# The head of a delta-rule and GELU kernel: a root on ScalarE, first squares on VectorE, unread products ahead of K, Q one tile ahead, loads in another order

## The chip, the core and the metric

The kernel runs on one core of a Trainium2 chip. The metric is the time of one execution on the device in microseconds (us); lower is better. The core has a matrix engine (TensorE, PE in the profile), a vector engine (VectorE, DVE), an engine for functions of one operand (ScalarE, ACT), a general one (GpSimd, POOL), and a queue that starts most transfers (SyncE, SP). Each engine takes its instructions in program order; semaphores order them between engines. Transfers run on 16 DMA engines.

## What is computed

```python
def _attn_ref(q, k, v, beta):                 # 4 x 8 heads, 768 tokens, 48 wide
    k_n = k / (np.linalg.norm(k, axis=-1, keepdims=True) + 1e-06)
    state = 0; y = 0
    for t in range(S):
        kt, vt, bt = (k_n[:, :, t], v[:, :, t], beta[:, :, t, None])
        y[:, :, t] = np.einsum('bhd,bhde->bhe', q[:, :, t], state)
        v_old = np.einsum('bhde,bhd->bhe', state, kt)
        state = state + bt[:, :, :, None] * np.einsum('bhd,bhe->bhde', kt, vt - v_old)
    return y

def _moe_ref(x, w_in, w_out):                 # x: 3072 tokens of 384; hidden 2048
    h = x @ w_in
    g = 0.5 * h * (1.0 + erf(h / sqrt(2)))
    return g @ w_out
```

q, k, v and beta are single precision. The two weight matrices come in double precision and are turned to single precision on the chip. The attention's output, with its heads joined, is the x of the second part.

## The kernel before

**Tiles.** The 768 tokens are cut into 12 chunks of 64 (`NC`, `C`). A unit (`tiles[c, a]`) holds chunk c of two batches, one in each half of the 128 partitions, all 8 heads side by side; a is 0 or 1, so there are two units a chunk. Two chunks form a group g, which is worked on as a whole where a small triangular system has to be inverted: the 64 x 64 block of a head is cut into 32 x 32 blocks, and the diagonal blocks are inverted by an elimination over 31 rows (`eliminate_steps`, L494).

**The head.** The first four units (`first`, chunks 0 and 1) are the first group. The order of their work is written out by hand on all five engines (L1189 to L1284); behind it a plan of due times (L1301 to L1425) orders VectorE and GpSimd. What happens, step by step:

- Loads: K of the four units, half of each on SP's queue and half on ScalarE's (L170, L171), then beta, then Q (L176), V of chunk 0 (`load_v(0)`, L1193), weight parts 0 and 1 (`fetch`, L1195), K of chunk 2 (`load_k`, L1196), and later Q of chunk 2, K of chunk 3, weight parts 2 and 3, the first three parts of the second matrix (L1232, into the `w_raw` slots) and V of chunk 1 (L1234).
- Norms: `squares` (L333) squares K and sums over 48 elements, on VectorE for three units and on GpSimd for one. `root` (L388) takes the square root of the 128 x 32 sums on VectorE: a start value out of the bits of the number and three Newton steps of three instructions. `factors` (L325) turns the root and beta into the factor `gm` of each token and head.
- K transposed (`transposed(u, (0,))`, L408): four TensorE transposes into PSUM and one ScalarE copy, L423. `diagonals` (L479) multiplies the transposed K with itself for the 32 x 32 diagonal blocks and copies them out on ScalarE (L492). `signs` (L1180) does the same for beta.
- `scales` (L498) transposes `gm` on VectorE (`gt`, L501) and spreads it on GpSimd into XM (L504). `flip` (L509) transposes the diagonal blocks of all four units into Nu (L511), and Nu is multiplied by XM (L516). The elimination, 58 small instructions on VectorE and some at its ends, works on Nu. Two transposes (`back`, L542 and L545) put the result into XM and Zf.
- While VectorE eliminates, TensorE and ScalarE do early work: `grams` (L448) of the four units, beta of the later chunks, Q transposed and `queries` (L466) for one unit after the other, then K transposed, grams and Q transposed for chunk 2 (`third`), and K and grams of chunk 3 (`fourth`). ScalarE also sums the squares of chunk 2 by head (`sum_of_squares`, L351: 16 instructions).
- After the elimination: `join` (L565) in two levels, `solve` (L776, products psU), `use` (L804, psY), `read`, `turn`, then the first products of the second part (`fc1`, L898, psH).

**Weights.** Sixteen parts are turned to single precision, each by `begin`, `exponents`, `mantissas` and `signed`. The exponent takes one of two forms (`two_kinks`, L240): one with two ScalarE passes and no sign step on VectorE, or one with a single ScalarE pass and one VectorE instruction more (L284). `signed` starts the transfer of the part that takes the freed place. There are four places for the parts of the first matrix (`NS`), and three for those of the second.

**Buffers.** PSUM tiles are "sq" (transposes, two buffers), "dn" (two of two banks each) and "mlp" (two).

Of the kernel before, what the change touches and what calls it, by code (L numbers as in the profile page):

```python
# [19 lines left out]
def kernel(  # L20
# [65 lines left out]
    lim = cpool.tile([128, 4], F32)  # L86
    for i, x in enumerate((-896.0 * 2 ** 23, 0.0, -896.0 - 1792.0 / 4095.0, 128.0 * 1792.0 / 4095.0)):
        nc.vector.memset(lim[:, i:i + 1], x)
# [69 lines left out]
    def load_v(c):  # L158
        if c >= NC:
            return  # L160
        for a in range(NA):
            u = tiles[c, a]
            u.V = io.tile([128, H, D], F32, tag="V", name="V", bufs=4)
            fetch_in(u.V, v, u)
# [17 lines left out]
    for i in range(NKS):  # L182
        nc.gpsimd.memset(Kp[i][:, :, D:], 0.0)
    mask = cpool.tile([128, C], F32)
    Gp = [cpool.tile([128, NA, NF, 128], F32, name=f"G{i}") for i in range(2)]
    G = Gp[0]
# [4 lines left out]
    nc.gpsimd.memset(mask, 1.0)  # L191
    nc.gpsimd.memset(low, 1.0)
    nc.gpsimd.affine_select(out=low, in_=low, compare_op=ALU.is_ge, fill=0.0, base=-1,
                            pattern=[[1, HB], [-1, HB]], channel_multiplier=0)
    for p in range(2):
        nc.gpsimd.affine_select(out=mask[HALF[p]], in_=mask[HALF[p]], compare_op=ALU.is_ge,
                                fill=0.0, base=-1, pattern=[[1, C]], channel_multiplier=-1)
    half = cpool.tile([128, NA * H], F32)
    nc.gpsimd.memset(half, 0.5)
    mask_h = mask.unsqueeze(1).to_broadcast([128, H, C])  # L200
    Zf = [cpool.tile([128, NU, C], F32, name="Zf")] * 2
    for p in range(2):
        nc.vector.memset(Zf[0][p * C + HB:(p + 1) * C, :, 0:HB], 0.0)
# [3 lines left out]
    nc.scalar.activation(lim[:, 1:2], lim[:, 0:1], ACT.Gelu)  # L207
# [32 lines left out]
    def two_kinks(n):  # L240

        return 0 < n < n_in or n_in + 3 < n < n_in + 7
# [79 lines left out]
    def new_group(g):  # L322
        gms[g] = wk.tile([128, 2 * NA, H], F32, tag="gm", name="gm")
# [9 lines left out]
    def squares(u, n, engine=None):  # L333
        kd = u.Kn[:, :, 0:D]
        if engine is nc.gpsimd:
            ksq = su.tile([128, H, D], F32, tag="w_e", name="ksq")
        elif engine is None:
            if u.c < 8:
                u.ksq = early_pair[u.a]
            else:  # L340
                if u.a == 0:
                    ns["ksq"] = more[0].tile([128, NA, H, D], F32, tag="TX", name="ksq")
                u.ksq = ns["ksq"][:, u.a]
            keep(nc.scalar.activation, u.ksq, kd, ACT.Square)
            return
        else:
            ksq = early_sq
        engine.tensor_tensor(ksq, kd, kd, op=ALU.mult)
        nc.vector.tensor_reduce(n, ksq, axis=AX.X, op=ALU.add)
# [12 lines left out]
    def norms(c):  # L362
        us = [tiles[c, a] for a in range(NA)]
        g = c // 2
        if c % 2 == 0:
            new_group(g)
        if c > 3 and c % 2 == 0:
            n = ns["pair"] = wk.tile([128, 2 * NA, H], F32, tag="n", name="n")
            ns[c], ns[c + 1] = n[:, 0:NA], n[:, NA:]
        for u in us:  # L370
            if c > 3:
                squares(u, None)
# [15 lines left out]
    def root(x):  # L388

        shape = list(x.shape)  # L390
        s = wk.tile(shape, F32, tag="root", name="root", bufs=1)
        r = wk.tile(shape, F32, tag="root_r", name="root_r", bufs=1)
        nc.vector.tensor_scalar(s.bitcast(U32), x.bitcast(U32), 0.5, 532487669.0,
                                op0=ALU.mult, op1=ALU.add)
        nc.vector.tensor_scalar_mul(x, x, 0.5)
        for i in range(3):
            nc.vector.reciprocal(r, s)
            nc.vector.tensor_tensor(r, r, x, op=ALU.mult)
            nc.vector.scalar_tensor_tensor(x if i == 2 else s, s, 0.5, r, ALU.mult, ALU.add)
# [603 lines left out]
    def keep(fn, *args, **kw):  # L1003
        i = fn(*args, **kw)  # L1004
        if free:
            tc.keep_in_program_order(i)
# [173 lines left out]
    def signs(c0, c1):  # L1180
# [11 lines left out]
        mybir.EngineType.PE, mybir.EngineType.SP}))  # L1192
    load_v(0)  # L1193
    for n in range(2):
        fetch(n)  # L1195
    load_k(2, "Kp")  # L1196
    new_group(0)
# [3 lines left out]
    for u in first:  # L1201
        squares(u, n0[:, u.t], nc.gpsimd if u.t == 1 else nc.vector)
        transposed(u, (0,))
        if u.t in (1, 2):
            diagonals(first[u.t - 2 + 1])
# [3 lines left out]
    root(n0)  # L1209
    scales_, flip_, *rows, back0, back1 = [s_[1:] for s_ in eliminate_steps(0)]  # L1210
    factors(gms[0], beta_m[:, 0:2].rearrange("q c a h -> q (c a) h"), n0)
    scales_[0]()
    flip_[0]()
# [3 lines left out]
    signs(2, NC)  # L1217
    third = [tiles[2, a] for a in range(NA)]
    sums_ = [(u, h) for u in third for h in range(H)]
    for u in first:  # L1220
        transposed(u, (1,))
        if u.c == 1:
            for x in sums_[5 * u.a:5 * u.a + 5]:
                sum_of_squares(*x)
        queries([u])
# [4 lines left out]
    for n in range(2, NS):  # L1230
        fetch(n)
    for n in range(n_in, n_in + len(slots)):  # L1232
        fetch(n)
# [3 lines left out]
    for x in sums_[10:13]:  # L1237
        sum_of_squares(*x)
# [3 lines left out]
    for x in sums_[13:]:  # L1242
        sum_of_squares(*x)
    fourth = [tiles[3, a] for a in range(NA)]
    for u in fourth:
        transposed(u, (0,))
    grams(fourth)
    for fn, *args in rows:
        fn(*args)
# [23 lines left out]
    signed(0)  # L1273
    begin(2)
# [183 lines left out]
```

## Time and profile before

| | |
|---|---|
| time, median of 3 runs | 631.01 us (629.24 to 631.15) |
| the profiled execution's own time | 630.75 us |
| its span, first to last instruction | 629.0 us |
| TensorE busy | 607.9 us, 97% of the span |
| VectorE, ScalarE, GpSimd busy | 428.0, 243.7, 209.7 us |
| mean granted TensorE clock of the span | 0.986 |
| GpSimd's first idle stretch before group 0's XM, and its next | 7.15 us, 23.34 us |

The page has a row of 40 slices for each engine, with the busy share of a slice in tenths, and a chain of waits, followed back from the last instruction to what released each. The timelines list one engine's instructions in order: start, duration, engine, line, operation, output and inputs, shape, count; brackets give the idle time ahead and what ended it. Where instructions of one kind are merged the duration is that of all. Two entries of TensorE stand for one single-precision product, and one for a transpose. The windows list each engine's busy time in a stretch, and then the clock, the DMA engines' share and their GB/s.

### The profile page before, as it was taken

Reading aid. Unit: us, or ns where it says so; the run is one execution under the profiler, and the core shown is the slowest. Engines: PE = TensorE matmul, PEld = TensorE weight load, DVE = VectorE, ACT = ScalarE, POOL = GpSimd, SP = SyncE. Lnnn points to the kernel's source line nnn. Section 1 sums busy time; section 2 is a strip of 40 time slices with the busy share of each in tenths; the row PEclk is TensorE's granted clock in tenths of the full one; section 3 lists DMA queues with packets and bytes.
Section 4 is the critical chain, followed back from the end, with each engine's and each line's share of the span. In section 5 each row is a group of like instructions: output and inputs, shape, how many; then the busy total and the mean of one; then the engine's idle time right before and its main releaser. Section 6 shows DMA issues by size and latency. Waiting matters only on the chain.

```text
span 629.0 us, 19679 instructions
## 1 busy us (share of the span) xinstructions
PE 607.9 (97%) x8358; PEld 541.0 (86%) x8358; DVE 428.0 (68%) x794; ACT 243.7 (39%) x549; POOL 209.7 (33%) x313
## 2 busy tenths in 40 slices
PE   6779999999999999999999999999999999999997
PEld 5667786676799999998899998899998899988997
DVE  7998899999867598564859555859545946332532
ACT  4577777615353156224451124451124222044200
POOL 4043001000369831786222884222884200000000
PEclk9986999999999999999999999999999999999999
DMA  9797556001433452363123533113321001000011
GB/s 133 161 285 194 114 130 188 14 12 37 69 41 51 74 93 35 54 121 37 17 40 49 98 72 39 13 29 64 67 50 17 12 3 27 5 22 1 0 26 26
DMA packets 159575, 39.63 MB, mean 63 GB/s; under 512 B 151168, under 2 KB 154368, under 8 KB 159488
## 3 DMA queue, kind: packets, MB, share of 16 engines
q1 hardware_dynamic: 156816, 37.34, 30.6%
q10 hardware_dynamic: 2672, 1.03, 0.8%
q8 instruction: 66, 1.08, 0.7%
q14 instruction: 21, 0.17, 0.1%
HBM read 33.62 MB, written 4.72 MB: 61 GB/s over the span
## 4 chain that ended last, share of the span: by engine, by line
PE 81%; DVE 13%; ACT 2%; DMA 2%; issue 1%; SPq 0%; DVEq 0%
PE psX L955 13%; PE psY L1021 11%; PE psY L955 9%; PE psX L1021 8%; PE psV L1021 5%; PE psZ L1021 5%; PE psZ L955 4%; PE psV L955 4%; DVE Nu L533 3%; DVE tmp L531 3%; PE psH L904 3%; PE psK L729 3%; PE psO L922 3%; PE psY L819 2%; PE psU L789 2%; PE psQ L749 2%
## 5 line engine op out<-in xcount | busy, mean ns | idle before, releaser
L380 POOL TENSOR_TENSOR n<-n,half 128x16 f32<-128x16 f32 x10 | 30.6, 3056 | 178.1 <-DVE n L378 118.4
L533 POOL TENSOR_TENSOR Nu<-Nu,tmp 128x30 f32<-128x30 f32 (+14 forms) x120 | 65.7, 548 | 9.4
L531 POOL TENSOR_TENSOR tmp<-Nu 128x30 f32<-128x30 f32 (+14 forms) x120 | 62.5, 520 | 9.4
L1021 PE MATMUL psX<-xT,w_in_sb 128*128 128x256 f32 (+1 forms) x288 | 62.5, 346 | 0.0
L955 PE MATMUL psX<-w_out_sb,G 128*128 128x192 f32 x320 | 56.4, 329 | 0.0
L955 PEld LDWEIGHTS psX<-w_out_sb,G 128*128 128x128 f32 x320 | 52.1, 190 | 0.8
L1021 PEld LDWEIGHTS psX<-xT,w_in_sb 128*128 128x128 f32 x288 | 47.9, 191 | 5.3
L904 PE MATMUL psH<-xT,w_in_sb 128*128 128x256 f32 x192 | 47.3, 400 | 1.4 <-ACT G L1004 1.3
L904 PEld LDWEIGHTS psH<-xT,w_in_sb 128*128 128x128 f32 x192 | 37.1, 199 | 9.5 <-ACT G L1004 2.1
L922 PE MATMUL psO<-w_out_sb,G 128*128 128x384 f32 x128 | 44.1, 490 | 0.1
L1049 DVE TENSOR_TENSOR psY<-psY,pu 128x512 f32<-128x512 f32 x20 | 14.0, 700 | 40.7 <-PE psY L1021 40.3
L1021 PE MATMUL psY<-xT,w_in_sb 128*128 128x256 f32 (+1 forms) x192 | 41.5, 345 | 0.0
L1004 ACT COPY xT<-psX 128x768 f32<-128x768 f32 x9 | 7.2, 799 | 81.8 <-PE psX L881 81.8
L1004 ACT COPY pu<-psZ 128x512 f32<-128x512 f32 x40 | 23.5, 586 | 38.7 <-PE psZ L1021 36.3
L922 PEld LDWEIGHTS psO<-w_out_sb,G 128*128 128x128 f32 x128 | 23.6, 190 | 14.4 <-issue 0.4
L1021 PEld LDWEIGHTS psY<-xT,w_in_sb 128*128 128x128 f32 x192 | 32.1, 191 | 3.5
L835 DVE TENSOR_TENSOR SQ<-SQ,psY 128x384 f32<-128x384 f32 x21 | 11.6, 553 | 32.5 <-PE psY L830 32.2
L1004 ACT ACTIVATE G<-G 128x512 f32<-128x512 f32 x40 | 25.2, 631 | 19.9 <-DVE G L1057 19.7
L1004 ACT ACTIVATE G<-psY 128x512 f32<-128x512 f32 x20 | 11.9, 596 | 47.3 <-PE psY L1021 47.3
L1057 DVE TENSOR_TENSOR G<-psY,pu 128x512 f32<-128x512 f32 x20 | 13.8, 690 | 22.2 <-PE psY L1021 21.5
L955 PE MATMUL psY<-w_out_sb,G 128*128 128x192 f32 x160 | 28.1, 329 | 0.0
L955 PE MATMUL psZ<-T,pu 128*128 128x192 f32 x160 | 28.1, 329 | 0.0
(206 smaller groups left out, 1373.8 us busy)
## 6 DMA issues: line engine op xcount, KB each, us to landing
Kp<-in_k_dram SPq DMA_DIRECT2D x76, 96.0 KB, 3.2
w_out_sb<-in_moe_w_in_dram SPq DMA_DIRECT2D x24, 256.0 KB, 4.9
w_raw<-in_moe_w_out_dram SPq DMA_DIRECT2D x16, 384.0 KB, 4.3
V<-in_v_dram SPq DMA_DIRECT2D x48, 96.0 KB, 3.0
out_dram<-o_sb SPq DMA_DIRECT2D x40, 96.0 KB, 2.2
Qp<-in_k_dram SPq DMA_DIRECT2D x64, 32.0 KB, 2.2
Qp<-in_q_dram SPq DMA_DIRECT2D x96, 16.0 KB, 2.0
Qp<-in_k_dram SPq DMA_DIRECT2D x64, 16.0 KB, 2.1
```

Source lines behind the costliest of these rows:

```text
L380: nc.gpsimd.tensor_tensor(flat, flat, half, op=ALU.pow)
L531: rows_on.tensor_tensor(tmp, nu[:, j + 1:, j:j + 1].to_broadcast([128, n, j]), nu[:, j:j + 1, 0:j].to_broadcast([128, n, j]), op=ALU.mult)
L533: rows_on.tensor_tensor(nu[:, j + 1:, 0:j], nu[:, j + 1:, 0:j], tmp, op=ALU.add)
L729: nc.tensor.matmul(u.psK[HALF[p], r, j, :], lhsT=u.Kt[rows, p, j, :], rhs=SQ[rows, u.a, p ^ r, j, 0:w], start=True, stop=True)
L749: nc.tensor.matmul(u.psQ[to, r, j, :], lhsT=u.Qt[rows, x, j, :], rhs=St[rows, u.a, p ^ r, j, :], start=True, stop=True)
L904: nc.tensor.matmul(psH, lhsT=w_in_sb[:, f // 2, m, f % 2 * 128:(f % 2 + 1) * 128], rhs=xTs[c][:, m, :], start=(m == 0), stop=(m == NM - 1))
L922: nc.tensor.matmul(u.psO, lhsT=G[:, u.a, f, :], rhs=w_out_sb[:, f, :], start=(f == 0), stop=(f == NF - 1))
L955: nc.tensor.matmul(ps_, lhsT=lhs[:, f, :], rhs=rhs[:, f, :], start=first and f == 0, stop=f == FH - 1, skip_group_check=not first)
L1004: i = fn(*args, **kw)
L1021: nc.tensor.matmul(ps_[:, i], lhsT=lhs[:, f // 2, f % 2 * 128:(f % 2 + 1) * 128], rhs=rhs, start=first and i == 0, stop=True, skip_group_c ...
L1049: nc.vector.tensor_tensor(L1["Y1"], L1["Y1"], L1["pu"][:, 0], op=ALU.add)
L1057: nc.vector.tensor_tensor(half(1, 1), shaped(L1["Y1"]), shaped(L1["pu"][:, 0]), op=ALU.add)
```

## The change

The sum of squares of the first four units is done by VectorE alone, with one reduction for the last two. The root is ScalarE's square root and one Newton step. ScalarE's function table is loaded for the root first, and for GELU behind the first grams. TensorE gets 28 products on a tile of zeros ahead of the first transposes, and two more behind the first unit's; nothing reads their result. Several memsets change engines. Q of a unit is transposed ahead of the queries of the unit before it, and beta of the later chunks ahead of the last queries. The 16 sums of squares of chunk 2 move behind. K of chunk 2 is loaded ahead of weight part 0, weight part 1 behind K of chunk 3, and the first parts of the second matrix behind `signed(0)`, some lines before the first product of `fc1`. Weight parts 1 and 2 take the form with one ScalarE pass.

```diff
@@ -83,8 +83,13 @@
-    lim = cpool.tile([128, 4], F32)
-    for i, x in enumerate((-896.0 * 2 ** 23, 0.0, -896.0 - 1792.0 / 4095.0, 128.0 * 1792.0 / 4095.0)):
+    Gp = [cpool.tile([128, NA, NF, 128], F32, name=f"G{i}") for i in range(2)]
+    G = Gp[0]
+    blank = G[:, 0, 0:4].rearrange("q f n -> q (f n)")
+    nc.vector.memset(blank, 0.0)
+    lim = cpool.tile([128, 5], F32)
+    for i, x in enumerate((-896.0 * 2 ** 23, 0.0, -896.0 - 1792.0 / 4095.0, 128.0 * 1792.0 / 4095.0,
+                           1e-30)):
         nc.vector.memset(lim[:, i:i + 1], x)
@@ -182,29 +187,21 @@
     for i in range(NKS):
         nc.gpsimd.memset(Kp[i][:, :, D:], 0.0)
     mask = cpool.tile([128, C], F32)
-    Gp = [cpool.tile([128, NA, NF, 128], F32, name=f"G{i}") for i in range(2)]
-    G = Gp[0]
     spare = Gp[1].rearrange("q a f n -> q (a f n)")
     low = spare[:, 0:HB * HB].rearrange("q (a b) -> q a b", b=HB)
     early_sq, *early_pair = [spare[:, HB * HB + i * H * D:HB * HB + (i + 1) * H * D].rearrange(
         "q (h d) -> q h d", d=D) for i in range(1 + NA)]
-    nc.gpsimd.memset(mask, 1.0)
-    nc.gpsimd.memset(low, 1.0)
-    nc.gpsimd.affine_select(out=low, in_=low, compare_op=ALU.is_ge, fill=0.0, base=-1,
-                            pattern=[[1, HB], [-1, HB]], channel_multiplier=0)
-    for p in range(2):
-        nc.gpsimd.affine_select(out=mask[HALF[p]], in_=mask[HALF[p]], compare_op=ALU.is_ge,
-                                fill=0.0, base=-1, pattern=[[1, C]], channel_multiplier=-1)
+    early_both = spare[:, HB * HB + H * D:HB * HB + (1 + NA) * H * D].rearrange("q (h d) -> q h d", d=D)
+    nc.vector.memset(mask, 1.0)
+    nc.vector.memset(low, 1.0)
     half = cpool.tile([128, NA * H], F32)
-    nc.gpsimd.memset(half, 0.5)
+    nc.vector.memset(half, 0.5)
     mask_h = mask.unsqueeze(1).to_broadcast([128, H, C])
     Zf = [cpool.tile([128, NU, C], F32, name="Zf")] * 2
-    for p in range(2):
-        nc.vector.memset(Zf[0][p * C + HB:(p + 1) * C, :, 0:HB], 0.0)
     SQ = cpool.tile([128, NA, 2, NP, D + C], F32, name="SQ")
     St = SQ[:, :, :, :, 0:D]
     nc.vector.memset(St, 0.0)
-    nc.scalar.activation(lim[:, 1:2], lim[:, 0:1], ACT.Gelu)
+    nc.scalar.activation(lim[:, 1:2], lim[:, 1:2], ACT.Sqrt)
     beta_m = cpool.tile([128, NC, NA, H], F32)
@@ -239,7 +236,7 @@
     def two_kinks(n):
-        return 0 < n < n_in or n_in + 3 < n < n_in + 7
+        return 2 < n < n_in or n_in + 3 < n < n_in + 7
     def high(e, dt):
@@ -330,23 +327,25 @@
         nc.vector.tensor_tensor(gm, bt_, r, op=ALU.mult)
         nc.vector.tensor_tensor(gm, gm, r, op=ALU.mult)
-    def squares(u, n, engine=None):
+    def squares(u):
         kd = u.Kn[:, :, 0:D]
-        if engine is nc.gpsimd:
-            ksq = su.tile([128, H, D], F32, tag="w_e", name="ksq")
-        elif engine is None:
-            if u.c < 8:
-                u.ksq = early_pair[u.a]
-            else:
-                if u.a == 0:
-                    ns["ksq"] = more[0].tile([128, NA, H, D], F32, tag="TX", name="ksq")
-                u.ksq = ns["ksq"][:, u.a]
-            keep(nc.scalar.activation, u.ksq, kd, ACT.Square)
-            return
+        if u.c < 8:
+            u.ksq = early_pair[u.a]
         else:
-            ksq = early_sq
-        engine.tensor_tensor(ksq, kd, kd, op=ALU.mult)
-        nc.vector.tensor_reduce(n, ksq, axis=AX.X, op=ALU.add)
+            if u.a == 0:
+                ns["ksq"] = more[0].tile([128, NA, H, D], F32, tag="TX", name="ksq")
+            u.ksq = ns["ksq"][:, u.a]
+        keep(nc.scalar.activation, u.ksq, kd, ACT.Square)
+
+    def first_squares(n):
+        for u in first:
+            kd = u.Kn[:, :, 0:D]
+            ksq = early_pair[u.a] if u.c else early_sq
+            nc.vector.tensor_tensor(ksq, kd, kd, op=ALU.mult)
+            if u.c == 0:
+                nc.vector.tensor_reduce(n[:, u.t], ksq, axis=AX.X, op=ALU.add)
+        nc.vector.tensor_reduce(n[:, NA:].rearrange("q a h -> q (a h)"), early_both, axis=AX.X,
+                                op=ALU.add)
     def sum_of_squares(u, h):
@@ -369,7 +368,7 @@
             ns[c], ns[c + 1] = n[:, 0:NA], n[:, NA:]
         for u in us:
             if c > 3:
-                squares(u, None)
+                squares(u)
     def prep(c):
         n = ns[c]
@@ -387,16 +386,13 @@
     def root(x):
-        shape = list(x.shape)
-        s = wk.tile(shape, F32, tag="root", name="root", bufs=1)
-        r = wk.tile(shape, F32, tag="root_r", name="root_r", bufs=1)
-        nc.vector.tensor_scalar(s.bitcast(U32), x.bitcast(U32), 0.5, 532487669.0,
-                                op0=ALU.mult, op1=ALU.add)
-        nc.vector.tensor_scalar_mul(x, x, 0.5)
-        for i in range(3):
-            nc.vector.reciprocal(r, s)
-            nc.vector.tensor_tensor(r, r, x, op=ALU.mult)
-            nc.vector.scalar_tensor_tensor(x if i == 2 else s, s, 0.5, r, ALU.mult, ALU.add)
+        s, r, h = (wk.tile(list(x.shape), F32, tag=t, name=t, bufs=1)
+                   for t in ("root", "root_r", "root_h"))
+        nc.scalar.activation(s, x, ACT.Sqrt, bias=lim[:, 4:5], scale=1.0)
+        nc.vector.tensor_scalar_mul(h, x, 0.5)
+        nc.vector.reciprocal(r, s)
+        nc.vector.tensor_tensor(r, r, h, op=ALU.mult)
+        nc.vector.scalar_tensor_tensor(x, s, 0.5, r, ALU.mult, ALU.add)
     def scale_head(u, h):
         nc.scalar.mul(u.V[:, h], u.V[:, h], ns[u.c][:, u.a, h:h + 1])
@@ -1190,61 +1186,77 @@
     by_hand.enter_context(tc.manual_schedule(engines={
         mybir.EngineType.DVE, mybir.EngineType.Pool, mybir.EngineType.Activation,
         mybir.EngineType.PE, mybir.EngineType.SP}))
+
+    def unread(n, cols):
+
+        psI = ps.tile([128, 512], F32, tag="mlp", name="psI")
+        for i in range(n):
+            nc.tensor.matmul(psI[:, 0:cols], lhsT=blank[:, 0:128], rhs=blank[:, 0:cols],
+                             start=True, stop=True)
+
+    third, fourth = [[tiles[c, a] for a in range(NA)] for c in (2, 3)]
+    for p in range(2):
+        nc.gpsimd.affine_select(out=mask[HALF[p]], in_=mask[HALF[p]], compare_op=ALU.is_ge,
+                                fill=0.0, base=-1, pattern=[[1, C]], channel_multiplier=-1)
+    nc.gpsimd.affine_select(out=low, in_=low, compare_op=ALU.is_ge, fill=0.0, base=-1,
+                            pattern=[[1, HB], [-1, HB]], channel_multiplier=0)
     load_v(0)
-    for n in range(2):
-        fetch(n)
     load_k(2, "Kp")
+    fetch(0)
     new_group(0)
     n0 = wk.tile([128, 2 * NA, H], F32, tag="n0", name="n0", bufs=1)
     for c in range(2):
         ns[c] = n0[:, c * NA:(c + 1) * NA]
-    for u in first:
-        squares(u, n0[:, u.t], nc.gpsimd if u.t == 1 else nc.vector)
-        transposed(u, (0,))
-        if u.t in (1, 2):
-            diagonals(first[u.t - 2 + 1])
+    first_squares(n0)
+    unread(28, 32)
+    transposed(first[0], (0,))
+    unread(2, 64)
+    transposed(first[1], (0,))
+    diagonals(first[0])
+    transposed(first[2], (0,))
+    diagonals(first[1])
+    transposed(first[3], (0,))
+    root(n0.rearrange("q a h -> q (a h)"))
     diagonals(first[2])
     signs(0, 2)
     diagonals(first[3])
-    root(n0)
     scales_, flip_, *rows, back0, back1 = [s_[1:] for s_ in eliminate_steps(0)]
     factors(gms[0], beta_m[:, 0:2].rearrange("q c a h -> q (c a) h"), n0)
     scales_[0]()
+    for p in range(2):
+        nc.gpsimd.memset(Zf[0][p * C + HB:(p + 1) * C, :, 0:HB], 0.0)
     flip_[0]()
     ng = wk.tile([128, NA, H], F32, tag="ng", name="ng", bufs=1)
     for u in first:
         grams([u])
-    signs(2, NC)
-    third = [tiles[2, a] for a in range(NA)]
+    nc.scalar.activation(lim[:, 1:2], lim[:, 0:1], ACT.Gelu)
     sums_ = [(u, h) for u in third for h in range(H)]
-    for u in first:
-        transposed(u, (1,))
-        if u.c == 1:
-            for x in sums_[5 * u.a:5 * u.a + 5]:
-                sum_of_squares(*x)
+    transposed(first[0], (1,))
+    for u, after in zip(first, first[1:] + [None]):
+        if after:
+            transposed(after, (1,))
+        else:
+            signs(2, NC)
         queries([u])
     for a in range(NA):
         fetch_q(tiles[2, a])
     for a in range(NA):
         fetch_in(Qp[2 + a][:, :, 0:D], k, tiles[3, a])
-    for n in range(2, NS):
-        fetch(n)
-    for n in range(n_in, n_in + len(slots)):
+    for n in range(1, NS):
         fetch(n)
     load_v(1)
     for u in third:
         transposed(u, (0,))
-    for x in sums_[10:13]:
+    for x in sums_[:8]:
         sum_of_squares(*x)
     grams(third)
     for u in third:
         transposed(u, (1,))
-    for x in sums_[13:]:
-        sum_of_squares(*x)
-    fourth = [tiles[3, a] for a in range(NA)]
     for u in fourth:
         transposed(u, (0,))
     grams(fourth)
+    for x in sums_[8:]:
+        sum_of_squares(*x)
     for fn, *args in rows:
         fn(*args)
     nc.vector.scalar_tensor_tensor(ng, gms[0][:, 0:NA], -1.0, ns[0], ALU.mult, ALU.mult)
@@ -1271,6 +1283,8 @@
     for u in first[:NA]:
         read(u)
     signed(0)
+    for n in range(n_in, n_in + len(slots)):
+        fetch(n)
     begin(2)
     mantissas(2)
     for u in first[:NA]:
```

## The prediction

> **What bounds the kernel now.** I read the page first, then the chain of waits from 0 to 90 us in order of time, then the timelines of the five engines for the first 62 us, and last the windows with the clock. The page's engine rows and slices:
>
> ```profile
> PE 607.9 (97%) x8358; PEld 541.0 (86%) x8358; DVE 428.0 (68%) x794; ACT 243.7 (39%) x549; POOL 209.7 (33%) x313
> PE   6779999999999999999999999999999999999997
> DVE  7998899999867598564859555859545946332532
> ```
>
> TensorE is busy 97% of the span and thin only in the first four of 40 slices, some 60 us. What the head loses, nothing later gives back: behind it TensorE is full. The chain says what sets the head:
>
> ```profile
> 10.74 0.82 PE psD L490 x53
> ...
> 13.64 0.38 ACT diag L492
> 14.02 0.02 issue
> 14.04 1.99 DVE Nu L511
> ...
> 41.23 1.84 DVE Zf L545
> ...
> 46.11 0.67 PE psU L789 x13
> 46.77 1.11 issue
> 47.89 1.62 PE psU L789 x38
> ```
>
> From 5.92 to 13.5 the chain is TensorE (K transposed, diagonal products), then the copy of the last diagonal block, and from 14.04 VectorE without a gap: flip, scaling at 16.13, elimination to 38.98, two transposes. At 46.77 TensorE stands 1.11 us for no operand at all. A second path into the scaling is nearly as late:
>
> ```profile
> 9.61 0.18 DVE L393 TENSOR_SCALAR root<-n 128x32 uint32<-128x32 uint32 x1
> 12.20 0.19 DVE L399 SCALAR_TENSOR_TENSOR n<-root,root_r 128x32 f32<-128x32 f32 x1
> 13.55 0.21 DVE L501 STREAM_TRANSPOSE gt<-gm 128x32 f32<-128x32 f32 x1
> 13.90 1.91 POOL L504 TENSOR_TENSOR XM<-G,gt 128x1024 f32<-128x1024 f32 x1 [7.15 <-DVE gt L501]
> ```
>
> Root 9.61 to 12.39, factors to 13.76, GpSimd's XM to 15.81; the flip ends at 16.03 and the scaling needs both. So the head gets shorter only if both paths do: the norms AND TensorE's diagonals.
>
> ```profile
> 4.41 1.09 PE L422 MATMUL psT<-ident,Kp 128*128 128x128 f32 x4 [4.41 <-DMA Kp<-in_k_dram]
> 18.40 1.27 PE L1183 MATMUL psB<-ident,w_in_sb 32*128 32x32 f32 x10
> 37.98 1.15 PE L422 MATMUL psT<-ident,Qp 128*128 128x128 f32 x8 [1.62 <-ACT SQ L423]
> ```
>
> The clock column calls the first 41 us full speed, but the same transposes took 0.21 each at 4.41 (1.09 less one's own 0.42, over 3) and about 0.13 at 37.98: the head's first 35 us ran at half clock. The column itself shows the next cold stretch:
>
> ```profile
> 44.00:46.10 2.10, 1.95 (x64) 1.87 (x65) 2.06 (x4) 1.34 (x3) 1.69 (x2) 0.50 1.03 399
> 60.00:64.00 4.00, 3.50 (x45) 2.75 (x44) 2.79 (x4) 3.79 (x6) 0.00 (x0) 1.00 0.91 247
> ```
>
> (the last three columns are granted clock, DMA share, GB/s.)
>
> **The change, part by part.** The sum is made against the profiled execution: span 629.0, its time 630.75, so 1.75 lie around the span; the median of the runs, 631.01, is 0.26 above it. 0.3%, about what a measurement here can tell from no change, is 1.9 us.
>
> *Root and squares.* The squares ended at 9.57. VectorE now does four products (0.56) and three reductions; the wide one, 768 elements, lies between 0.55 and twice that. The last K pair was read at 8.43, so the norms are whole between 9.3 and 10.1: nothing gained, I take 9.6. The root loses the bit trick, the halving from the path, and two of three Newton steps (0.84 each, 9.92 to 10.75). It gains one ScalarE pass on 128x32 (0.25, the row of 128x48) and two handovers of about 0.05: 2.78 becomes 0.35 + 0.80 = 1.15, if ScalarE is free. The first table load (1.28 at 3.63) is now the root's and costs what it cost. ScalarE is not always free: the pass stands behind the fourth K copy (L423, 0.59), and behind it wait two diagonal copies (0.37 each) and beta's two (0.40).
>
> *Unread products.* 28 products of 128 weight columns on 32, then 2 on 64. Single-precision products leave two records each (12 for the 6 of psH in the chain). The nearest row is psB: 128 columns loaded for 32 streamed, (1.27 - 0.29)/9 = 0.109 a record at half clock. So 56 x 0.109 = 6.1 us at half clock, 3.0 at full. They start at about 1.5, behind a memset of 512 (0.47, from 0.70 for 768). The first K transposes, which started at 4.41, are queued behind them: 7.6 if the clock never rises, 6.2 to 7.6 if it rises underway. This is the price. The return is a full clock for what follows: in the chain from 5.92 to 13.5 TensorE did 3 transposed tiles (1.04), 4 diagonals (0.82), beta 0.35 and an issue gap of 0.52.
>
> [...]
>
> What raised the clock here was denser: 31.0 to 36.4, full transposes and 64-wide products back to back, and the psH products from 54.9. [...] Whether loading counts, no row says: both ends stay. I take "it rises", the more likely by little, and near 6.2, since behind the dense psH products, begun at 54.92, it rose after 4.7 us (the window 55 to 60 has 0.53, so near 59.7). Then 44 records fit before the switch and 12 at half the pitch behind it.
>
> *Then the K stage.* Unread end 6.8; T0 to 7.4, the 2 fillers 0.25, T1 to 8.2, each tile then 0.55 + 0.45 on TensorE but 0.59 + 0.37 plus handovers on ScalarE, which becomes the pace: fourth K copied at 10.8 (before 11.37), root pass to 11.1, gt at 11.15 + 0.80 + 1.34 = 13.3 (before 13.76), XM to 15.35, scaling 15.4 instead of 16.13: **-0.7**. [...]
>
> *Work off the path.* Q one tile ahead removes up to 4 gaps of 0.68 on TensorE before 31, and the second table load (1.28, row L207) delays the first Q copy behind two Q transposes; cover: TensorE's early work ended at 40.93, 0.45 before the join needed it, and the saved gaps keep that cover. With no cover 1.28 would show. The sums of squares, 16 of 0.23, leave the Q stage for two blocks of 8 (1.84), behind third and fourth tile; the last ends near 41, when the Zf copies need ScalarE. Zf's memset on GpSimd, 2 x 0.91, stands behind XM, where GpSimd idled 23.3 us. Mask and low: memsets moved to VectorE, 1.1 for the 1.82 of Zf taken away.
>
> *Loads.* On SP the 4 K loads pass 6 weight issues; 3 of the weight issues move behind 12 q and k issues; the 6 w_raw issues (2.36 MB) move from 37.3 to behind weight part 4 near 52. V(1), 4 issues, thereby lands about ten us earlier than 50.1, where GpSimd got it. Parts 5 to 7 come up to 6 later (2.36 MB at the window's 399 GB/s): part 5 was issued at 53.3 and first read at 68.88, so still hidden; without that slack up to 6. w_raw itself is first read at 81.70. With less traffic at 45 (1.03 of the engines in the window above) I expect the 1.11 issue gap at 46.77 to shrink: -1.1 to 0. Against it: scale_v (2.48) on GpSimd now follows the masking at 45.7 and lies beside the Zf copies (L590); VectorE's L284 took 1.59 beside it instead of 0.95, so up to 0.6 comes back. Net **-0.6**, bounds -1.1 to +0.6.
>
> *Two weights of the other form.* Parts 1 and 2 cost VectorE 0.95 more each and ScalarE one pass fewer (about 2.1 to 0.94). VectorE waited 1.07, 0.41 and 1.18 for exactly those passes at 55.5 to 62.6: nothing, 0; without these waits +1.9.
>
> *Clock at the join.* TensorE idles longer before 39, so the first join (1.51, part of it at full clock) may take psJ's cold 1.95: **+0.4**, bounds 0 and 0.4. [...]
>
> Sum: -0.7 - 0.6 + 0.4 = -0.9, so 629.85 on the profiled scale; I say **629.7**, own range 628.3 to 630.9.
>
> **Rivals.** [...]
>
> *The clock stays down* (other side). Place: the 56 weight loads ahead of T0. T0 at 7.6, then 1.05, fillers 0.44, T1 to 10.1, two pairs of diagonal and transposed tile (0.82 + 1.04) to 13.8, K copy to 14.5, root pass 14.7, gt 16.9, XM to 18.95: scaling at 19.0 instead of 16.13, +2.9; with the loads' -0.6 and the join as before, 633.0 to 633.6, I take 633.3. It decides as soon as T0 starts past about 6 without a raised clock. For it: 6.26 us of busy TensorE did not raise it.
>
> *Decoding binds.* If VectorE has no wait to hide the two extra passes: 629.7 + 1.3 = 631.0. For it: VectorE is 8 to 9 tenths busy there; against: the 1.18 wait.
>
> **Numbers.** Forecast 0.42, both win 0.20, clock down 0.32, decoding 0.06. Faster by over 0.3% (below 629.1): 0.20 + 0.15 of the forecast's low part = 0.35. Slower (above 632.9): 0.30 of the third. Same: 0.35. Range: 627.8 to 633.5, which takes in both other ends. As both signs carry weight, the likeliest case's own range is the 628.3 to 630.9 above.
>
> **What would show it.** T0's start (6.2 to 7.6) and the pitch of the transposes and diagonals behind the unread products: 0.11 a transpose is the forecast, 0.21 the other side. The scaling's start (15.4; 19.0). No gap in psU near 45. XM of group 0 ready before the early work ends would show the Q stage as cover lost. Wrong altogether if weight parts 5 to 7 make VectorE wait for DMA at 65 to 76, or if unread products take 0.1 each from the start.

## The result: 641.48 us, slower by 1.75%

After takes 641.48 us (median of 4 runs, 640.75 to 641.76), before took 630.43 beside it (4 runs, 629.24 to 631.15): a ratio of 1.0175, 95% interval 1.0155 to 1.0196, some 11 us. The forecast was 629.7, its range 627.8 to 633.5: the change went the other way, past the end of the range. The profiled execution of after took 641.7, its span is 639.9 against 629.0.

The engine row of the page of after, and its slices of TensorE and VectorE:

```profile
PE 618.4 (97%) x8418; PEld 553.1 (86%) x8418; DVE 427.2 (67%) x792; ACT 243.1 (38%) x550; POOL 208.6 (33%) x311
...
PE   9876998999999999999999999999999999999997
DVE  4699888999868578854876834968744946332532
```

TensorE has 60 records more and 10.5 us more of busy time. Its first slices, thin before (6, 7, 7), are now 9, 8, 7, and VectorE's first slice fell from 7 to 4: TensorE is busy where VectorE waits for it. The chain of waits of after (start, duration, what) shows at what:

```profile
1.52 12.15 PE psI L1194 x56
13.67 0.91 PE psT L418 x4
...
19.95 0.59 ACT Kt L419
20.54 0.23 ACT root L391
20.79 0.36 DVE root_r L393
...
23.11 1.93 POOL XM L500
25.06 1.24 DVE Nu L512
...
50.09 1.85 DVE Zf L541
...
57.25 1.96 PE psU L785 x64
```

The unread products (psI) are the first link of the chain on TensorE and, at 12.15 us, the longest of the whole chain. Both paths into the scaling stand behind them: the diagonals, and the root, whose pass on ScalarE waits behind the copy of the fourth transposed K tile. The scaling of L512 starts at 25.06 instead of 16.13: 8.93 later. Elimination, transposes and joins carry that delay on; the first hidden-layer product (psH) starts at 64.54 instead of 54.92, and 80 us into the run TensorE stands 8.6 behind. Behind the head two smaller sums are added, which the timeline of after shows (start, busy time, engine, line, operation, idle time before it and what ended it):

```profile
20.79 0.35 DVE L393 RECIPROCAL root_r<-root 128x32 f32<-128x32 f32 x1 [10.64 <-ACT root L391]
...
103.23 0.56 DVE L253 TENSOR_SCALAR w_e<-w_raw 128x768 uint32<-128x768 uint32 x1 [1.34 <-DMA w_raw<-in_moe_w_out_dram]
...
107.70 0.56 DVE L250 TENSOR_SCALAR w_e<-w_raw 128x768 int32<-128x768 int32 x1 [0.58 <-DMA w_raw<-in_moe_w_out_dram]
...
110.18 2.20 PE L918 MATMUL psO<-w_out_sb,G 128*128 128x384 f32 x6 [1.61 <-DVE w_out_sb L282]
...
333.80 0.45 PE L439 MATMUL psG<-Kt 48*64 48x64 f32 x13 [0.94 <-issue]
```

The timelines of before have in the same places:

```profile
16.13 1.22 DVE L516 TENSOR_TENSOR Nu<-Nu,XM 128x1024 f32<-128x1024 f32 x1
...
107.20 0.56 DVE L256 TENSOR_SCALAR w_e<-w_raw 128x768 uint32<-128x768 uint32 x1 [0.71 <-DMA w_raw<-in_moe_w_out_dram]
...
322.23 1.16 PE L443 MATMUL psG<-Kt 48*64 48x64 f32 x64
```

VectorE waits twice for w_raw in after, 1.92 us together, and once in before, 0.71; and TensorE waits for VectorE. The distance between the two kernels, record against record of TensorE, goes from 8.6 at 80 us to 10.5 at 100 and falls back to 9.6 by 200. And at 333.80 TensorE stands 0.94 us for nothing that the profile shows, in the middle of 64 like products that ran through in before: 9.6 becomes 10.9, and so it stays to the end. So 8.6 from the head, 1.0 around w_raw and 1.3 at that stop make the 10.9 by which the two spans differ. Three windows of after, the columns as in those of before, show a cold clock at the join again and its later return:

```profile
53.00:55.00 2.00, 1.92 (x64) 1.78 (x64) 1.96 (x3) 0.94 (x3) 2.00 (x3) 0.50 0.04 8
60.00:64.00 4.00, 3.77 (x76) 2.90 (x73) 3.84 (x6) 3.21 (x11) 0.00 (x0) 0.50 0.35 104
68.00:72.00 4.00, 4.00 (x48) 3.02 (x46) 3.93 (x6) 3.23 (x5) 0.00 (x0) 1.00 1.02 389
```

In before the clock was full again from 59.66, here from 67.20: 7.5 later, less than the head's delay. So its return adds nothing of its own to the time.

### The profile page after: what moved, and what is told of

The parts are those of the page before. It is cut to its first block, busy times and chain, and to the rows that moved or that the text cites. A ratio compares the mean times of both kernels' runs of the same rounds, so it can differ in the third digit from the quotient of the medians.

```text
span 639.9 us, 19800 instructions
## 1 busy us (share of the span) xinstructions
PE 618.4 (97%) x8418; PEld 553.1 (86%) x8418; DVE 427.2 (67%) x792; ACT 243.1 (38%) x550; POOL 208.6 (33%) x311
## 4 chain that ended last, share of the span: by engine, by line
PE 82%; DVE 12%; ACT 2%; issue 2%; DMA 1%; POOL 0%; SPq 0%; DVEq 0%; POOLq 0%
PE psX L951 12%; PE psY L1017 11%; PE psY L951 8%; PE psX L1017 8%; PE psV L1017 6%; PE psZ L1017 5%; PE psZ L951 4%; PE psV L951 4%; DVE Nu L529 3%; DVE tmp L527 3%; PE psK L725 3%; PE psH L900 3%; PE psO L918 3%; PE psY L815 2%; PE psI L1194 2%; PE psU L785 2%
## 5 line engine op out<-in xcount | busy, mean ns | idle before, releaser
L900 PE MATMUL psH<-xT,w_in_sb 128*128 128x256 f32 x192 | 45.9, 392 | 1.4 <-ACT G L1000 1.3
L951 PE MATMUL psY<-T,G 128*128 128x192 f32 x160 | 28.1, 329 | 0.0
```

The costliest lines, as they stand in the source:

```text
L900: nc.tensor.matmul(psH, lhsT=w_in_sb[:, f // 2, m, f % 2 * 128:(f % 2 + 1) * 128], rhs=xTs[c][:, m, :], start=(m == 0), stop=(m == NM - 1))
L951: nc.tensor.matmul(ps_, lhsT=lhs[:, f, :], rhs=rhs[:, f, :], start=first and f == 0, stop=f == FH - 1, skip_group_check=not first)
```

## Experiments

Eleven kernels were run. Times are medians; a ratio is to before on the same chip, with its 95% interval.

**Is it the unread products?** Take them out of after, or put them alone into before.

```
# e1_no_unread: after
-    unread(28, 32)
-    unread(2, 64)
# e2_before_unread: before, with the memset of blank
+    unread(28, 32)         ahead of the first K transpose
+    unread(2, 64)          ahead of the second
```

> The changed kernel without its 28 and 2 unread products. Theory A (their 60 entries hold TensorE until 13.5 and everything behind moves by that): the first K transposes start at 4.4 again, the scaling of Nu at 15.6 to 16.2 instead of 25.06, and the time falls by about 9, to 632.5 (631.5 to 633.3). Rival B (the ScalarE root behind the copies, the second table load and the moved loads cost most of it, TensorE only waits with them): the scaling stays behind 20 and the time above 637.

> The kernel before with the unread products alone (28 of 32 columns ahead of the first transposes, 2 of 64 behind the first unit's, and the memset of their tile). Theory A: the first transposes start near 13.5, the scaling near 25, the time is 639.5 (638.8 to 640.5). Rival B: under 634, since the rest of the head is as before.

Without them after took 631.42 us (10 runs, ratio 1.003, 1.0018 to 1.0043): 10.06 less by the medians, 9.1 by the two ratios. Before with them took 639.94 (1.016, 1.0142 to 1.0179): 9.96 more than the 629.98 beside it. So the block alone accounts for 9 to 10 of the 11 us, added or taken away. In e1_no_unread the first K transposes start at 4.51 again; the scaling starts at 16.97, not by the expected 16.2.

**What sets its price?** A record of the unread products took 0.213 us at half clock, where the forecast had 0.109. Three kernels vary the streamed columns, the weight columns and the rows:

```
# e3_dense: after
-    unread(28, 32)
+    unread(28, 128)
# e5_cols64: after
-            nc.tensor.matmul(psI[:, 0:cols], lhsT=blank[:, 0:128], rhs=blank[:, 0:cols],
+            nc.tensor.matmul(psI[0:64, 0:cols], lhsT=blank[:, 0:64], rhs=blank[:, 0:cols],
# e6_rows32: after
-            nc.tensor.matmul(psI[:, 0:cols], lhsT=blank[:, 0:128], rhs=blank[:, 0:cols],
+            nc.tensor.matmul(psI[:, 0:cols], lhsT=blank[0:32, 0:128], rhs=blank[0:32, 0:cols],
```

> The changed kernel with 28 products on 128 columns instead of 32, the same number of weight loads. [...] Rival D (products on zeros or with no reader do not raise the clock): the block ends at 13.5 as before or later, 0.21 a transpose, 641.5 within 1.

> After with the weights of the 30 unread products narrowed from 128 columns to 64; number of products, streamed columns and rows as in after. Theory (the weight load sets the pitch, in proportion to the columns loaded): 0.107 us a record at half clock instead of 0.213, the block of 56 from 1.5 to about 7.5, the first K transpose at 7.5 instead of 13.48, the clock still down through the K stage, the scaling near 19.5, and the time 641.5 - 6 = 635.5 (634.5 to 636.5). Rival (each single-precision product has a fixed price, whatever it loads): pitch 0.213, first transpose at 13.5, time 641.5.

> After with the unread products reduced to 32 of the 128 rows (the shared dimension), 128 weight columns kept. The row of beta's transposes, from which the prediction took 0.109 a record, has 32 rows as well, so rows could be what made it cheap. Theory (columns and the form decide, rows do not): pitch 0.213 at half clock, first K transpose at 13.5, time near 641.5. Rival (rows decide): pitch 0.109 or less, first K transpose near 7.6, time near 635.5.

e3_dense, with four times the streamed columns, was faster than after: 637.16 (1.013, 1.0099 to 1.0161). Rival D, 641.5 within 1, is out; the author's own estimate was records of 0.213 still and 3 to 6 less than 641.5, and it is 4.3. Its timeline of TensorE:

```profile
7.74 3.18 PE L1194 MATMUL psI<-G 128*128 128x128 f32 x27
10.75 0.60 PE L418 MATMUL psT<-ident,Kp 128*128 128x128 f32 x4
...
14.67 0.29 PE L486 MATMUL psD<-Kt 48*32 48x32 f32 x16
16.27 0.61 PE L486 MATMUL psD<-Kt 48*32 48x32 f32 x48 [1.31 <-issue]
```

Up to 7.59 its records took 0.213 like those with 32 columns, so streaming does not set the price. Then the clock rose, 6.07 after the first product, and 27 records took 3.18 (0.112 each), and the transposes behind took 0.60 for four instead of 1.09. In after, e2_before_unread and e6_rows32, 12.15 us of products with 32 columns, without a gap, did not raise it. What e3_dense streams is zeros as well. Here is one line of the timelines of e5_cols64 and of e6_rows32:

```profile
1.52 6.18 PE L1194 MATMUL psI<-G 128*64 128x32 f32 x56 [1.52 <-DVE lim L93]
```

```profile
1.52 12.15 PE L1194 MATMUL psI<-G 32*128 32x32 f32 x56 [1.52 <-DVE lim L93]
```

Half the weight columns take half the time (0.107 a record), and a quarter of the rows changes nothing (12.15 as in after). With 64 columns the first K transposes (T0 of the prediction) started at 7.63, the scaling at 19.62, and the time was 637.29 (1.0122, 1.0105 to 1.0138), 1.8 above the 635.5 expected from the head alone and past the end of its range, 636.5. e6_rows32 took 643.63 in its one run, 2 above the expected 641.5; its pitch and its first K transposes, at 13.60, were as its theory had them.

**The rest of the change.**

```
# e4_loads_back: e1_no_unread, w_raw as in before
+    for n in range(n_in, n_in + len(slots)):     ahead of load_v(1)
+        fetch(n)
-    for n in range(n_in, n_in + len(slots)):     ahead of begin(2)
-        fetch(n)
```

> As e1_no_unread, and the first three parts of the second matrix are loaded where they were in the kernel before, ahead of V of chunk 1. Theory E (with them behind weight part 4 the SP queue is late for the parts that follow, and VectorE waits 1.3 and 0.6 for them near 103 and 107): no such wait over 0.8, and 1 to 2 us less than e1_no_unread, near 631. Rival F (these waits only fill time that TensorE's work sets): the same as e1_no_unread within 0.6.

It took 630.75 (10 runs, 1.0006, 0.9993 to 1.0018): 0.67 less than e1_no_unread by the medians, 1.5 by the two ratios. VectorE waits for w_raw three times in the timeline of e1_no_unread (0.77, 0.62 and 1.17) and once in that of e4_loads_back, 0.95 at 107.55. That one is longer than theory E allowed, and 0.67 is just outside rival F: the old place of w_raw is better, but by how much is not settled. The profiled execution of e1_no_unread took 634.32, the slowest of its ten. All else in the change, root, squares, Q ahead, memsets and the two weight parts, together is worth nothing that can be measured. Why the root gained nothing can be seen in the timeline of e4_loads_back:

```profile
11.83 0.35 DVE L393 RECIPROCAL root_r<-root 128x32 f32<-128x32 f32 x1 [1.72 <-ACT root L391]
...
14.73 1.97 DVE L507 STREAM_TRANSPOSE Nu<-diag 128x1024 f32<-128x1024 f32 x1 [0.72 <-ACT diag L488]
```

The norms were whole at 9.9, but ScalarE's pass stood behind the fourth K copy until 11.48: these 1.6 us ate the 1.6 that the shorter root was to save (2.78 less 1.15). And the flip waits for the last diagonals anyway.

**Does a raised clock help, if it costs nothing?** In e7_short the unread products are dense and short and run while K lands; e8_short_root also puts the root's pass ahead of the copy.

```
# e7_short: e4_loads_back
+    unread(7, 128)
     transposed(first[0], (0,))
+    unread(2, 128)
# e8_short_root: e7_short
-    transposed(first[3], (0,))
     root(n0.rearrange("q a h -> q (a h)"))
+    transposed(first[3], (0,))
```

> After with the unread products made short and dense: 7 of 128 streamed columns ahead of the first K transpose and 2 of 128 between the first and the second (in place of 28 of 32 and 2 of 64), and the four w_raw parts put back ahead of V(1) on SP. 14 records of 0.213 fill 1.5 to 4.5, the time in which K lands anyway; the 4 fillers take 0.85 of a gap of 0.5. [...] Rival 1 (the stretch is too short or the gaps spoil it): clock stays down, the scaling at 16.8 to 17.2 as without unread products, time 630.5 to 631.3. Rival 2 (a faster K stage only meets longer issue gaps): clock up, the scaling still at 16.5 or later, time 630 to 631.

> As e7_short, with the root's pass on ScalarE put ahead of the copy of the fourth K tile instead of behind it. Theory (in after's order the one pass waits 1.5 behind a copy that waits for TensorE): the pass starts near 10.0 to 10.3 instead of 11.5, gt near 12.3 to 12.6 instead of 13.8, XM ends near 14.5; with the diagonals also done by then the scaling starts at 14.6 to 15.3, time 628.0 to 629.3. Rival (TensorE's diagonals and their copies set the scaling alone): gt is early, the scaling is where e7_short has it, and the time the same within 0.3.

They took 631.98 (12 runs, 1.0024, 1.0008 to 1.0039) and 632.49 (1.0034, 1.0022 to 1.0046): both a little slower than before. Timeline of e7_short, TensorE:

```profile
6.07 0.63 PE L418 MATMUL psT<-ident,Kp 128*128 128x128 f32 x4
...
9.18 0.71 PE L486 MATMUL psD<-Kt 48*32 48x32 f32 x58
12.33 0.32 PE L486 MATMUL psD<-Kt 48*32 48x32 f32 x6 [2.44 <-issue]
...
48.54 0.32 PE L571 MATMUL psJ<-Zf,XM 32*32 32x32 f32 x4 [2.39 <-issue]
```

The first K transposes started at 4.67 (before 4.41), the clock was up from 5.21, and a tile's transposes took 0.63 instead of 1.09: the aim of the change, reached at 0.26 of delay. The author's estimate for this run, with the clock up near 7.6 as in e3_dense, was a scaling at 15.3 to 16.2 and 628.8 to 630.2. But then TensorE stood 2.44 us in the middle of the third tile's diagonals, and the scaling started at 16.41 (before 16.13). Rival 2 of the expectation comes nearest: a raised clock and no earlier scaling; but 16.41 and 631.98 both lie outside its numbers. A second stop, 2.39, came four records before the end of the second join. In e8_short_root the root's pass ran at 10.16, and nothing came of it: beta's transposes lay behind the first stop, 2.69 there, the factors waited 2.17 for them, gt came at 14.54 and the scaling at 16.85. Neither its theory nor its rival, which both had gt early, foresaw this.

**What the stops are.** Counted in TensorE's records, those of before lie as follows (its timeline):

```profile
11.49 0.42 PE L1183 MATMUL psB<-ident,w_in_sb 32*128 32x32 f32 x2
11.84 0.34 PE L490 MATMUL psD<-Kt 48*32 48x32 f32 x10
12.70 0.81 PE L490 MATMUL psD<-Kt 48*32 48x32 f32 x54 [0.52 <-issue]
13.44 2.39 PE L443 MATMUL psG<-Kt 48*64 48x64 f32 x74
16.70 1.76 PE L443 MATMUL psG<-Kt 48*64 48x64 f32 x54 [0.88 <-issue]
```

Four tiles' transposes (16), three tiles' diagonals (192), 2 of beta and 10 of the fourth tile: it stands after 220 records, and again after 54 + 74 = 128 more. In e7_short, 18 + 16 + 128 + 58 = 220. In all thirteen traces TensorE stands after 220 and after 348 records, whatever lies there, 0.3 to 2.7 us. In six of them a third stop comes after 849 or 850: in before it is the 1.11 in psU, in e7_short the 2.39 in the second join. The trace's records of instruction transfers show one of 16,384 bytes that starts before each: in e7_short it began at 9.39, TensorE went on at 12.33; in before 9.80 and 12.70. In all traces TensorE goes on 2.2 to 3.1 us after that start. The two longest of the first stops, 2.44 and 2.69, are those of e7_short and e8_short_root, which ran up to it at raised clock. To test the count, records were added or moved:

```
# e9_phase: e8_short_root
-    unread(7, 128)
+    unread(4, 128)
     transposed(first[0], (0,))
-    unread(2, 128)
+    unread(1, 128)
...
+    signs(0, 2)
     diagonals(first[2])
-    signs(0, 2)
# e10_order_alone: e9_phase
-    unread(4, 128)
     transposed(first[0], (0,))
-    unread(1, 128)
# e11_before_shift: before, with the memset of blank
+    unread(6, 32)          ahead of the first K transpose
```

> As e8_short_root, with beta's two transposes ahead of the third tile's diagonals and 5 unread products (4 and 1, 10 records) instead of 9 (18 records). Theory (TensorE's instructions come in blocks: in every trace read so far it stands at its 220th record and again each 128 later, whatever they compute, so the records ahead only shift which work the stop falls into): 10 + 16 + 2 + 3 x 64 = 220, so the first stop falls between the third and the fourth tile's diagonals; the second join's stop (2.4 to 2.5 at 60 of 64 records of psJ in e7_short) moves 8 records on, to the 4th record of psU. The scaling at 15.4 to 16.2, the time 629.2 to 630.9. Rival (the stops are waits for data and stay with their instructions): the stop again inside the third tile's diagonals, psJ's last four late by 2.4, time 632.

> As e9_phase without any unread product: root's pass ahead of the fourth K copy, beta's transposes ahead of the third tile's diagonals, w_raw as before. Theory (without a raised clock and with the stop at its 220th record inside the fourth tile's diagonals, the flip sets the scaling, not the root): gt early, 12.2 to 12.7, and yet the scaling at 16.6 to 17.0 as in e4_loads_back, time 630.3 to 631.0. Rival (the root set it): the scaling at 15.5 to 16, time 629.5 to 630.0.

> Before with 6 unread products of 32 columns (12 records of 0.213, done at 4.1, ahead of K's landing at 4.4) and the memset of their tile. Theory (blocks of instructions): the stops of before at record 220 (10 records into the fourth tile's diagonals, 0.52) and in psU (13 records in, 1.11) move 12 records earlier, to the end of the third tile's diagonals and to the first record of psU; the work itself costs nothing, time 630 to 631.5. Rival (stops stay with their instructions): diagonals split 10 and 54, psU 13 and 51 as in before, time 630.5.

Timeline of e11_before_shift, TensorE:

```profile
10.74 0.88 PE L492 MATMUL psD<-Kt 48*32 48x32 f32 x64
12.89 0.31 PE L1185 MATMUL psB<-ident,w_in_sb 32*128 32x32 f32 x2 [1.27 <-issue]
...
47.05 0.31 PE L791 MATMUL psU<-V,Zf 64*64 64x48 f32 x1 [0.67 <-issue]
48.41 1.96 PE L791 MATMUL psU<-V,Zf 64*64 64x48 f32 x63 [1.05 <-issue]
...
416.07 0.33 PE L445 MATMUL psG<-Kt 48*64 48x64 f32 x3 [0.97 <-issue]
```

Both stops moved by exactly the 12 records: from the fourth tile's diagonals to the end of the third's, in psU from 13 to 1. The 0.67 ahead of that one record is not explained by the count. And 400 us later a stop stands in the Gram products where before has none. The time was not the expected 630 to 631.5 but 632.18 (6 runs, 1.0035, 1.0019 to 1.0051): before with 12 unread records, done ahead of K's landing, and their memset is 2.3 us slower. The profiled execution took 630.62, 1.6 under the median, so its trace does not show all of that, and where the rest went stays open.

e9_phase had its stop between third and fourth diagonals, where expected. Its timeline of TensorE:

```profile
11.36 0.89 PE L486 MATMUL psD<-Kt 48*32 48x32 f32 x64
13.32 0.89 PE L486 MATMUL psD<-Kt 48*32 48x32 f32 x64 [1.07 <-ACT diag L488]
```

The profile puts this one down to ScalarE's copy of a diagonal block; but the last such copy had ended at 12.66, 0.66 before TensorE went on, and the transfer had begun at 10.46, 2.86 before. The clock did not rise before 31.8, the scaling started at 16.79, and the time was 632.25 (1.0043, 1.0028 to 1.0058), both above their ranges. e10_order_alone took 630.43 (10 runs, 1.0007, 0.999 to 1.0023), as its theory had it. Its timeline of VectorE:

```profile
12.67 0.21 DVE L497 STREAM_TRANSPOSE gt<-gm 128x32 f32<-128x32 f32 x1
14.53 1.96 DVE L507 STREAM_TRANSPOSE Nu<-diag 128x1024 f32<-128x1024 f32 x1 [1.65 <-ACT diag L488]
16.60 1.23 DVE L512 TENSOR_TENSOR Nu<-Nu,XM 128x1024 f32<-128x1024 f32 x1
```

Here the root's saving is real, gt is 0.9 earlier than in before, and worth nothing: the flip starts at 14.53, behind diagonals in which TensorE stood 0.91 us after its 220th record. So in this order TensorE's diagonals, with the stop in them, set the scaling, and not the root. What it would be without the stop no run shows, since every run has it.

The late stop of after fits the same reading. The traces were laid beside that of before, record by record of TensorE. Those with 60 records ahead (after, e2, e3, e5, e6) fall back by 1.0 to 2.1 us at one place, 323 us on before's time, and all five stand there after 4913 records. Those with 10 to 18 (e7, e8, e9, e11) fall back by 0.9 to 1.3 near 416, after 6183 or 6184 records; those with none (e1, e4, e10) at neither. Each of these nine stops ends 2.3 to 2.6 us after the start of a 16,384-byte instruction transfer. In these traces the place goes with how many records stand ahead, not with what they compute: after, e3, e5 and e6 differ in columns and rows and stand after the same 4913. None of the versions was faster than before.

## Why the prediction was wrong

**What bounds the kernel** was read rightly. The head passes its delay on almost whole, 8.93 at the scaling and 8.6 at 80 us, and both paths into the scaling had to win; e10_order_alone shows one of them winning alone, for nothing.

**The unread products: the step that failed.** "56 x 0.109 = 6.1 us" should have been 56 x 0.213 = 12. The 0.109 came from psB's row, a transpose of 128 weight columns; a product that loads as many columns takes twice that (0.213; e6_rows32 excludes the rows as the reason, e5_cols64 shows the price in proportion to the columns, 0.107 for 64). Why psB's transposes came at half that time no run here tells. The 6.1 was called "the price" and given no upper end above it, though the row was of another kind of instruction. One was at hand: the prediction itself read 0.21 a record off the K transposes at 4.41, with 128 weight columns too, and 56 x 0.21 is 11.8. The kernel's own small products were no better measure than psB: psG in before (54 records in 1.76) takes 0.027 a record for 64 weight columns, where the unread products of e5_cols64 take 0.107.

**"It rises, near 6.2"** failed too: 12.15 us did not raise the clock, nor had 6.26 us without a gap in before, from 5.92 to 12.18: its Gram products at 16.70 (54 in 1.76) still ran at nearly twice the time of those at 39.75 (64 in 1.18). For a rise soon after the start, on which the 6.2 at the lower end of T0, the 0.20 for both paths and with them the 627.8 rested, no run with 32 streamed columns gives a figure; with 128 the clock was up 3.69 us (e7_short) and 6.07 us (e3_dense) after the first product. The doubt was put rightly (whether loading counts), and e3_dense answers it for these products: with 128 streamed columns for 128 loaded the clock rose, with 32 it did not, though the records came every 0.213 in both. At 0.213 a record for the 0.109 reckoned with, the products also streamed only half as many columns in a us. The rival "the clock stays down" had the mechanism, at 633.3, with T0 at 7.6 where it was 13.48: the same 0.109, mis-sized. e5_cols64 is that rival at its own price, T0 at 7.63 and the scaling at 19.62 (19.0 was worked out), and took 637.29, not 633.3. So the rival's sum was 4 too low even where its T0 was right. The trace of e5_cols64 says why: at 80 us 2.75 of the delay are left, near the 2.9 worked out, but w_raw adds 1.0 in place of the -0.6, and the stop at 323 adds 2.1.

**Root and squares.** "If ScalarE is free" was the condition, and it was not: the pass waited behind the fourth K copy. Where the pass was freed (e10_order_alone), the saving of the path still came to nothing: the diagonals were late, with an issue gap of 0.91 in them.

**Loads, "net -0.6".** Wrong in sign: w_raw in its new place costs 0.67 between the medians of e1_no_unread and e4_loads_back, 1.5 by their ratios, and 1.0 in the trace of after. That the weight parts would come "up to 6 later" and stay hidden left out that the later w_raw parts are issued behind the queue's other loads as well: in after the seventh w_raw transfer was issued at 97.47, in before at 85.07, 12.4 apart where the head is 8.6 behind, and VectorE waited for it.

**Two weights at 0, Q ahead at 0, the join +0.4:** e4_loads_back, which keeps these and the root, the squares and the rest of the loads, lies -0.4 to +1.1 us from before. That bears out their sum; the single terms were not measured.

**Issue gaps** were named three times (0.52, 0.88, 1.11) and treated as local. A gap like them took back the gain of the K stage in e7_short, and the 60 new records brought one up at 323 us: 1.3 of the 11 us, at a place the prediction did not look at.

## What to carry to other kernels

Price an added instruction from a row of the same kind, and where there is none, take the dearest of the near rows as an upper end: here 0.21 stood beside 0.109. Filler work that stands in front of real work on an in-order engine must be shorter than the wait it fills (here 12.15 us stood where K lands at about 4.5), counted in the worst clock (0.213 a record, not 0.112); and even where it was (e11_before_shift), the kernel came out 2.3 us slower. Before paying for a faster engine, look at what stops it for no operand: here stops at a fixed count of TensorE's records, up to 2.69 us, took back all that a raised clock gave. Records added ahead move the work that a later stop falls into, so an edit in the head can cost a microsecond 300 us behind it (1.3 in after, near 323 on before's time), and comparing two kernels record by record finds it.

## What the runs showed of the hardware

- A single-precision product of 128 weight columns leaves two records of 0.213 us each before the clock rose, for 32 streamed columns (after) as for 128 (e3_dense), and of 0.112 behind the rise (e3_dense); with 64 weight columns 0.107, the clock still down (e5_cols64). "Half clock" for the head is read from this pitch. A transpose with 128 weight columns and 32 streamed took 0.109 (before).
- TensorE stopped after its 220th and 348th record in every trace, 0.3 to 2.7 us, each time 2.2 to 3.1 us behind the start of a 16,384-byte instruction transfer. 128 records lie between the two stops, but no stop follows at each further 128: before and after have 66 such transfers each and ran through their 476th and 604th record.
- The clock rose under dense streaming of zeros (128 streamed columns for 128 loaded: e3_dense at 7.59, e7_short at 5.21), and not under 12.15 us of sparse products (32 for 128) without a gap (after, e2_before_unread, e6_rows32). Its steps lie 3.41 us or multiples of it apart (in after 39.89, 46.72, 67.20), and where they fall differs between executions with the same work: e7_short and e8_short_root start alike and rose at 5.21 and 6.84; after and e2_before_unread have the same records up to 17 us, and e2_before_unread rose at 17.01 for 3.41 us, after not before 39.89. So each of these is one execution's clock. e9_phase, with 8 fewer unread records than e7_short, got no raised clock in the K stage; e11_before_shift, with 12 sparse ones, got one at 11.47 for 3.41 us.
- The clock column reads 1.00 ahead of the first clock record, while the K transposes there took 0.21 a record in before and after; at raised clock (e7_short) they took about 0.11.
